# Packed attention and two expert layers on one core: a shorter float64 conversion and a four-turn attention pipeline

## The chip, the cores and the metric

The kernel runs on one core of one Trainium2 chip. The metric is the device time of one execution in microseconds (us). Engines are named as the profile names them: PE (TensorE), DVE (VectorE), ACT (ScalarE), POOL (GpSimd) and SP (SyncE, which issues the transfers). Each works through its own instructions in order and waits on semaphores for the others.

## What is computed

Three blocks in a row: attention over 32 learned queries p, a dense two-layer block with squared ReLU, and a block of eight experts of which each token takes one. The shapes are B = 8, H = 8, S = 576, D = 64 (4608 tokens of 512 values), `w_in` 512x2048, `w_out` 2048x512.

```python
def sm_attn(qq, kk, vv):
    s = scale * np.matmul(qq, kk.transpose(0, 1, 3, 2))
    s = s - np.max(s, axis=-1, keepdims=True)
    a = np.exp(s)
    a = a / (np.sum(a, axis=-1, keepdims=True) + 1e-09)
    return np.matmul(a, vv)
p_packed = sm_attn(p, k, v)
out = sm_attn(q, p_packed, p_packed)
x = out.transpose(0, 2, 1, 3).reshape(B * S, H * D)
h = np.maximum(x @ w_in, 0.0)
x = (h * h) @ w_out
# then: e = argmax(x @ w_gate + modality_bias), out = gate * (relu(x @ w1[e]) @ w2[e])
```

`w_in` and `w_out` arrive as float64. Each value is two 32-bit words, an upper (`top`: sign, exponent, the upper part of the fraction) and a lower one (`low`). The chip's engines work in float32, so the kernel puts each float32 together from these two words.

## The kernel before

**Stages.** A start loop takes 16 quads of heads through the first attention (`att1`: scores L297, maximum L308, exponential L310, normalisation L315, transposes L320/L321, their copies `atbuf` L322/L323, products `pq` L329/L330, results to `pp32` and split into two halves for PE by ACT L346 and POOL L347). Beside it 16 conversions turn `w_in` into `wbt`, and `pw_unit` (PE L361, copied out by DVE L365 or ACT L367, for the first pair split again by ACT L376 and POOL L377) multiplies the packed values with `w_in`. Then `others(u)` makes the rest of these products and converts `w_out`, one of 16 blocks per call, into the places of `wbt` that fall free. From there twelve units u of 384 tokens run, each with 16 steps f: `layer1` (PE L474, or L480/L482/L483 with DVE L487 for the four units that lie in two batches; then ACT L489 to L491 and a subtraction L493 make the two halves `ghl`), and `layer2` (PE L500, nine matmuls a step). The gate (L521) and the routing run behind them, and then the expert block, which the change does not touch.

**Conversion.** `convert` uses a scratch of two halves, m and tf, of which there are three, so conversion i takes the scratch that conversion i-3 used. In tf the float32 is built; ACT rounds it into the high half (L215), and POOL subtracts for the low half (L216). The raw words lie in three or four buffers; the transfer for a later block starts when the last DVE instruction that reads the buffer is done.

**Second attention.** `att2(u)` is a generator: for each of three tiles of 128 tokens it computes scores (PE L428) and subtracts the maximum (DVE L439), turn; exponential (ACT L443), sum and reciprocal (DVE L445 to L447) and multiplication (POOL L448) on the buffer `e`, of which there is one, turn; two transposes (PE L455) and the split into `a2T` (ACT L458, DVE L459), turn. In the units, `bga = Paced([att2(u + 1)], R_ATT)` takes R_ATT turns of it in each of the 16 steps.

**What sets the order.** The code is written in program order, and a planner arranges each engine's instructions by that order, by priorities (`CHAIN` puts L486 to L493 forty places ahead) and by a timeline that it simulates. So where an instruction stands on its engine can't be read from the code; the orders below are those of the built programs. Line numbers of the changed kernel are 2 lower from the end of `convert` on, and 1 lower from the new `yield` on; in its `convert`, L202 is the first ACT instruction, L203 the new maximum, L204 the mask and shift, L213 and L214 are what were L215 and L216.

Of the kernel before, what the change touches and what calls it, by code (L numbers as in the profile page):

```python
# [10 lines left out]
F32 = mybir.dt.float32  # L11
# [4 lines left out]
AF = mybir.ActivationFunctionType  # L16
ALU = mybir.AluOpType
# [2 lines left out]

P = 128
EPS = 1e-9
MIN_NORMAL = float(np.array([897 << 20], np.int32).view(np.float32)[0])


@with_exitstack
def tile_pack_attention_moe_moe2(
# [15 lines left out]
    nc = tc.nc  # L43
# [153 lines left out]

    def convert(sc, raw, hi, lo):
        top, low = raw[:, :, 1], raw[:, :, 0]
        m, tf = sc[:, :512], sc[:, 512:]  # L200
        t = tf.bitcast(I32)
        nc.scalar.activation(out=m, in_=top.bitcast(F32), func=AF.Square)  # L202
        nc.vector.tensor_scalar(  # L203
            out=t, in0=top, scalar1=0x07FFFFFF, scalar2=3, op0=ALU.bitwise_and, op1=ALU.logical_shift_left  # L204
        )
        nc.vector.scalar_tensor_tensor(
            out=t, in0=top, scalar=-0x40000000, in1=t, op0=ALU.bitwise_and, op1=ALU.bitwise_or
        )
        nc.vector.scalar_tensor_tensor(
            out=t, in0=low, scalar=29, in1=t, op0=ALU.logical_shift_right, op1=ALU.bitwise_or  # L210
        )
        nc.vector.scalar_tensor_tensor(
            out=tf, in0=m, scalar=MIN_NORMAL * MIN_NORMAL, in1=tf, op0=ALU.is_ge, op1=ALU.mult  # L213
        )  # L214
        nc.scalar.activation(out=hi, in_=tf, func=AF.Copy)  # L215
        nc.gpsimd.tensor_tensor(out=lo, in0=tf, in1=hi.bitcast(F32), op=ALU.subtract)  # L216
# [12 lines left out]
    def conversions(srcs, raws, scs):  # L229
        n = len(raws)  # L230

        def load(i):
            if i < NU:
                nc.sync.dma_start(raws[i % n].bitcast(I32).rearrange("p (f t) -> p f t", t=2), srcs[i])

        for i in range(n):
            load(i)
        for i in range(NU):
            w = wbt[:, i]
            raw = raws[i % n].bitcast(I32).rearrange("p (f t) -> p f t", t=2)  # L240
            convert(scs[i % len(scs)], raw, w[:, 0, :], w[:, 1, :])
            load(i + n)
            yield
# [12 lines left out]
    def bank(tag, name):  # L256
        if "early" in held:
            return held["early"].tile([P, 512], F32, tag="e", name=name, bufs=4)
        return held["all"].tile([P, 512], F32, tag=tag, name=name, bufs={"acc": 3, "h": 2, "t": 3}[tag])
# [148 lines left out]
    def parts(t0, n):  # L408
        got, t = [], t0
        while t < t0 + n:  # L410
            b = t // S
            e = min(t0 + n, (b + 1) * S)
            got.append((b, t - t0, e - t))
            t = e
        return got

    def att2(u):
        hl = held["at"].tile([P, 2, NPC, UW], F32R, tag="a2T", name="a2T", bufs=2)
        a2T[u] = hl
        for r in range(UT):  # L420
            t0 = u * UW + r * P
            c0 = r * P
            qT = held["at"].tile([P, HP, P], F32, tag="qT", name="qT", bufs=2)
            nc.sync.dma_start(qT, qT_d[:, t0 : t0 + P].rearrange("(g p) t -> p g t", p=P))
            s2 = bank("t", "s2")
            for b, off, n in parts(t0, P):
                for g in range(HP):
                    nc.tensor.matmul(  # L428
                        s2[off : off + n, g * 64 : (g + 1) * 64],
                        qT[:, g, off : off + n],  # L430
                        pp32[:, b, g, :],
                        start=True,
                        stop=True,
                    )
            s2v = s2[:, : H * NPK].rearrange("p (h n) -> p h n", h=H)
            mx = held["at"].tile([P, H], F32, tag="mx", name="mx", bufs=2)
            nc.vector.tensor_reduce(out=mx, in_=s2v, axis=AX.X, op=ALU.max)
            e = held["at"].tile([P, H, NPK], F32, tag="e", name="e", bufs=1)
            nc.vector.tensor_tensor(  # L439
                out=e, in0=s2v, in1=mx.unsqueeze(2).to_broadcast([P, H, NPK]), op=ALU.subtract  # L440
            )
            yield
            nc.scalar.activation(out=e, in_=e, func=AF.Exp, scale=SCALE)  # L443
            sm = held["at"].tile([P, H], F32, tag="sm", name="sm", bufs=2)
            nc.vector.tensor_reduce(out=sm, in_=e, axis=AX.X, op=ALU.add)  # L445
            nc.vector.tensor_scalar(out=sm, in0=sm, scalar1=EPS, scalar2=None, op0=ALU.add)
            nc.vector.reciprocal(out=sm, in_=sm)  # L447
            nc.gpsimd.tensor_tensor(  # L448
                out=e, in0=e, in1=sm.unsqueeze(2).to_broadcast([P, H, NPK]), op=ALU.mult
            )  # L450
            yield
            ta = bank("t", "ta2")
            ef = e.rearrange("p h n -> p (h n)")
            for c in range(NPC):
                nc.tensor.transpose(ta[:, c * P : (c + 1) * P], ef[:, c * P : (c + 1) * P], ident)  # L455
            tv = ta[:, : NPC * P].rearrange("p (c n) -> p c n", c=NPC)
            hi = hl[:, 0, :, c0 : c0 + P]
            nc.scalar.activation(out=hi, in_=tv, func=AF.Copy)  # L458
            nc.vector.tensor_tensor(out=hl[:, 1, :, c0 : c0 + P], in0=tv, in1=hi.bitcast(F32), op=ALU.subtract)  # L459
            yield  # L460
# [418 lines left out]
                    split_pw(b, i)  # L879


    R_ATT = 0.75
    pT_v = pT_d.rearrange("p (b g n) -> p b g n", b=B, g=HP)
    nc.sync.dma_start(pn[:, :2], pT_v[:, :2])
    load_k(0)
# [9 lines left out]
    for i in range(len(quads) + 3):  # L895
        if i < len(quads):
            runs.append(att1(i))
        for r in (runs if i < 3 else runs[:1] + runs[:0:-1]):
            with tc.high_priority(offset=PRI):
                next(r)  # L900
        if i >= 3:
            runs.pop(0)
        if i == A20:
            bg = [att2(0)]
        pull(bg)
        pull(cv, 2)
        if i == 8:
            pull(cv, NU)
            held["head"] = const.tile([P, HEAD, 2, NPC, P], F32R, tag="head", name="head")
        for bp, u in PW.get(i, ()):  # L910
            pw_unit(bp, u)
# [54 lines left out]
    for u in range(NUN):  # L966
        pair, k = divmod(u, UPP)
        last = u == NUN - 1
        if u == 1:
            st1.close()  # L970
            nc.sync.dma_start(
                wgb.rearrange("p e d -> p (e d)"), w_gateT.rearrange("e d -> (e d)").partition_broadcast(P)
            )
            held["xg"] = ctx.enter_context(tc.tile_pool(name="xg", bufs=2, side="right"))
        bga = Paced([] if last else [att2(u + 1)], R_ATT)
        for f in range(NF):
            hl = layer1(u, f)
            if pend is not None:
                second_layer()
            pend = (u, f, hl)  # L980
            if f == 0:
                gens, n = background(u)
                bgt = Paced(gens, n / ((NF - 6 if last else NF) - 1.5))
            if u == 0:
                others(f + AHEAD)
            bga.step()
            bgt.step()
            ahead(pair, k, f)
            if last and f == NF - 6:
                bgt.finish()  # L990
                bgt = Paced([weights1(0)], 1)
        bga.finish()
        bgt.finish()
# [74 lines left out]
```

## Time and profile before

| | |
|---|---|
| median of 3 runs | 1283.46 us (1280.68 to 1285.04) |
| the profiled execution | 1291.58 us |
| its span, first to last instruction | 1289.7 us |
| PE busy | 1235.6 us, 96% |
| DVE busy | 834.3 us, 65% |
| ACT busy | 633.3 us, 49% |
| POOL busy | 325.2 us, 25% |

The profiled execution took 0.6% longer than the median, and 1.9 us of its time lie outside its span. PE is busy nearly everywhere, but not at the same pace: in the page's forty slices the granted clock of TensorE is 0.6 to 0.7 of full speed in the first four and 0.8 or more in the others. A busy share counts what an engine is occupied with, also where an instruction takes longer because something else stands in its way.

### The profile page before, as it was taken

To read this page: it belongs to the slowest core of one execution; us is meant where nothing else is said; L and a number is where in the kernel's file an instruction comes from. 1 tells how busy PE (TensorE), PEld (TensorE's weight loads), DVE (VectorE), ACT (ScalarE), POOL (GpSimd) and SP (SyncE) were. 2 spreads that over 40 slices of the span, in tenths; PEclk is the share of its full clock that TensorE was granted. 3 is DMA by queue.
4 is the path that set the end of the run, shared out by engine and by line. 5 is a ranking of instruction groups with operands and counts; after the bars stand their busy time and mean duration, and the time that the engine had idled before them with its cause. 6 is when DMAs were issued, how large, how long until landed. Compare 5 with 4: busy or idle time off the path is not lost.

```text
span 1289.7 us, 18073 instructions
## 1 busy us (share of the span) xinstructions
PE 1235.6 (96%) x6100; PEld 1021.7 (79%) x6100; DVE 834.3 (65%) x2168; ACT 633.3 (49%) x1337; POOL 325.2 (25%) x389
## 2 busy tenths in 40 slices
PE   7898989899999999999999999999999999999995
PEld 5566878688888888888888888878787888888884
DVE  4877676687685985779597497988643454354331
ACT  3556466466546765456754576642332333343230
POOL 3644365332101222013221023101220121122011
PEclk6777999999999999999999999999999999999998
DMA  9875665621111222012220112341542442353210
GB/s 335 281 267 185 185 180 176 180 83 50 59 50 33 67 74 67 9 53 74 64 72 20 43 40 87 99 156 42 181 135 90 170 167 97 131 182 115 97 66 36
DMA packets 74167, 145.04 MB, mean 112 GB/s; under 512 B 6608, under 2 KB 26192, under 8 KB 73936
## 3 DMA queue, kind: packets, MB, share of 16 engines
q1 hardware_dynamic: 68304, 124.62, 29.8%
q0 software_dynamic: 5760, 19.17, 4.6%
q8 instruction: 50, 0.82, 0.3%
q14 instruction: 53, 0.43, 0.1%
HBM read 109.92 MB, written 33.85 MB: 111 GB/s over the span
## 4 chain that ended last, share of the span: by engine, by line
PE 74%; DVE 10%; DMA 6%; issue 4%; ACT 2%; POOL 2%; SPq 0%; POOLq 0%; DVEq 0%; ACTq 0%
PE acc L500 24%; PE o L809 13%; PE h L787 12%; PE ph L474 9%; DMA wraw<-in_moe_w 3%; DVE rows L521 3%; PE pq L329 3%; PE pw L361 2%; PE s L428 2%; PE s L297 1%; PE ph L482 1%; PE ph L483 1%; PE ph L480 1%; PE tr L767 1%; DMA wgb<-in_moe_w_gate 1%
## 5 line engine op out<-in xcount | busy, mean ns | idle before, releaser
L500 PE MATMUL acc<-wbt,ghl 128*128 128x512 f32 x1728 | 446.0, 399 | 2.6 <-ACT ghl L491 2.3
L500 PEld LDWEIGHTS acc<-wbt,ghl 128*128 128x128 f32 x1728 | 319.5, 189 | 64.4 <-ACT ghl L491 4.3
L521 DVE SCALAR_TENSOR_TENSOR rows<-rows,wgb 128x512 f32<-128x512 f32 x288 | 213.8, 742 | 6.8 <-DMA wgb<-in_moe_w_gate 3.4
L787 PE MATMUL h<-xt,wbt 128*128 128x512 f32 x864 | 214.2, 398 | 0.4 <-DVE xt L771 0.4
L787 PEld LDWEIGHTS h<-xt,wbt 128*128 128x128 f32 x864 | 162.2, 189 | 39.6 <-DVE xt L771 0.9
L493 DVE TENSOR_TENSOR ghl<-r,ghl 128x384 fp32r<-128x384 f32 x176 | 107.0, 610 | 78.2 <-ACT ghl L491 76.4
L491 ACT ACTIVATE ghl<-r 128x384 fp32r<-128x384 f32 x192 | 99.9, 521 | 82.7 <-PE acc L500 80.8
L820 POOL DMA_INDIRECT out<-wgb,idx_s x36 | 39.2, 1088 | 341.1 <-DVE wgb L818 251.4
L798 DVE SCALAR_TENSOR_TENSOR ht<-h,ht 128x512 fp32r<-128x512 f32 x72 | 48.8, 687 | 113.3 <-ACT ht L797 112.2
L809 PE MATMUL o<-head,ht 128*128 128x512 f32 x432 | 113.8, 398 | 4.8 <-ACT ht L797 4.5
L809 PE MATMUL o<-ring,ht 128*128 128x512 f32 x432 | 111.5, 394 | 0.0
L797 ACT ACTIVATE ht<-h 128x512 fp32r<-128x512 f32 x72 | 42.0, 592 | 140.2 <-PE h L787 139.9
L490 ACT ACTIVATE r<-r 128x384 f32<-128x384 f32 x192 | 99.7, 523 | 4.1
L809 PEld LDWEIGHTS o<-head,ht 128*128 128x128 f32 x432 | 80.6, 189 | 24.7 <-ACT ht L797 5.8
L809 PEld LDWEIGHTS o<-ring,ht 128*128 128x128 f32 x432 | 80.5, 188 | 17.0
L489 ACT ACTIVATE r<-ph 128x384 f32<-128x384 f32 x128 | 61.9, 486 | 63.2 <-PE ph L474 34.7
L405 POOL TENSOR_TENSOR ring<-praw,ring 128x256 fp32r<-128x256 f32 x62 | 51.1, 825 | 156.3 <-ACT ring L404 138.4
L474 PE MATMUL ph<-a2T,ring 128*128 128x384 f32 x420 | 85.6, 339 | 0.0
L474 PEld LDWEIGHTS ph<-a2T,ring 128*128 128x128 f32 x420 | 74.7, 188 | 4.8
L724 DVE TENSOR_TENSOR wbt<-wraw,wbt 128x1024 fp32r<-128x1024 f32 x36 | 44.0, 1223 | 51.0 <-ACT wbt L723 50.5
L474 PE MATMUL ph<-a2T,head 128*128 128x384 f32 x348 | 72.5, 340 | 0.0
L448 POOL TENSOR_TENSOR e<-e,sm 128x256 f32<-128x256 f32 x36 | 28.7, 797 | 171.1 <-DVE sm L447 164.6
(225 smaller groups left out, 1860.3 us busy)
## 6 DMA issues: line engine op xcount, KB each, us to landing
wraw<-in_moe_w SPq DMA_DIRECT2D x72, 512.0 KB, 3.6
praw<-pw_d SPq DMA_DIRECT2D x56, 256.0 KB, 3.8
pw_d<-pws SPq DMA_DIRECT2D x48, 256.0 KB, 3.2
x_d<-rows SPq DMA_DIRECT2D x12, 792.0 KB, 4.2
qT<-in_q SPq DMA_DIRECT2D x36, 256.0 KB, 3.0
early<-in_v SPq DMA_DIRECT2D x16, 512.0 KB, 5.5
rows<-in_k SPq DMA_DIRECT2D x10, 576.0 KB, 7.0
wgb<-in_moe_w_out SPq DMA_DIRECT2D x11, 512.0 KB, 4.1
```

The lines of the kernel that those rows point to most:

```text
L405: nc.gpsimd.tensor_tensor(out=t[:, 1], in0=raw, in1=t[:, 0].bitcast(F32), op=ALU.subtract)
L474: nc.tensor.matmul(ph, t[:, x, c, :], a[:, y, c, :], start=(i == 0), stop=(i == 3 * NPC - 1))
L489: nc.scalar.activation(out=r, in_=ph if len(ps) == 1 else r, func=AF.Relu)
L490: nc.scalar.activation(out=r, in_=r, func=AF.Square)
L491: nc.scalar.activation(out=hl[:, 0], in_=r, func=AF.Copy)
L493: eng.tensor_tensor(out=hl[:, 1], in0=r, in1=hl[:, 0].bitcast(F32), op=ALU.subtract)
L500: nc.tensor.matmul(acc[t], hl[:, x, t * P : (t + 1) * P], wbt[:, f, y, :], start=(f == 0 and x == 0 and y == 0), stop=(f == NF - 1 and x = ...
L521: nc.vector.scalar_tensor_tensor(out=junk, in0=row[:, t, :DM], scalar=1.0, in1=wgb[:, e], op0=ALU.mult, op1=ALU.mult, accum_out=one)
L724: nc.vector.tensor_tensor(out=t[:, 1, :], in0=raw, in1=t[:, 0, :].bitcast(F32), op=ALU.subtract)
L787: nc.tensor.matmul(ph, half1[:, g % 2, c, x, f * P : (f + 1) * P], xs[c][:, y, :], start=(i == 0), stop=(i == 3 * NDC - 1),)
L798: nc.vector.scalar_tensor_tensor(out=h[:, 1, :], in0=ph, scalar=0.0, in1=h[:, 0, :].bitcast(F32), op0=ALU.max, op1=ALU.subtract)
L809: nc.tensor.matmul(po, hs[f][:, x, t * P : (t + 1) * P], second(f)[:, y, :], start=(i == 0), stop=(i == 3 * NFE - 1),)
```

## The change

Three edits. In `convert`, ACT writes the absolute value of the upper word (read as a float) into tf, where it wrote the square into m; a new DVE instruction takes the maximum of that and a constant (in place); the mask and shift now read tf in place of the strided upper word; and the last DVE instruction, which multiplied the result by a comparison of the square with a limit, is dropped. So DVE still has four instructions for a block, a maximum in place of the comparison, and ACT's comes at the head of the chain. In `att2` a second `yield` stands between the multiplication and the transposes, so a tile has four turns and not three. `R_ATT` goes from 0.75 to 0.95 turns a step.

```diff
-MIN_NORMAL = float(np.array([897 << 20], np.int32).view(np.float32)[0])
+TOP_MIN = float(np.array([896 << 20], np.int32).view(np.float32)[0])
...
-        m, tf = sc[:, :512], sc[:, 512:]
+        tf = sc[:, 512:]
         t = tf.bitcast(I32)
-        nc.scalar.activation(out=m, in_=top.bitcast(F32), func=AF.Square)
+        nc.scalar.activation(out=tf, in_=top.bitcast(F32), func=AF.Abs)
+        nc.vector.tensor_scalar(out=tf, in0=tf, scalar1=TOP_MIN, scalar2=None, op0=ALU.max)
         nc.vector.tensor_scalar(
-            out=t, in0=top, scalar1=0x07FFFFFF, scalar2=3, op0=ALU.bitwise_and, op1=ALU.logical_shift_left
+            out=t, in0=t, scalar1=0x07FFFFFF, scalar2=3, op0=ALU.bitwise_and, op1=ALU.logical_shift_left
         )
...
-        )
-        nc.vector.scalar_tensor_tensor(
-            out=tf, in0=m, scalar=MIN_NORMAL * MIN_NORMAL, in1=tf, op0=ALU.is_ge, op1=ALU.mult
         )
         nc.scalar.activation(out=hi, in_=tf, func=AF.Copy)
...
                 out=e, in0=e, in1=sm.unsqueeze(2).to_broadcast([P, H, NPK]), op=ALU.mult
             )
+            yield
             yield
             ta = bank("t", "ta2")
...
-    R_ATT = 0.75
+    R_ATT = 0.95
```

The first place is ACT during the conversions of `w_in`, where the fifth block is worked on (`stage`, `wgb` and `extra` are raw buffers and scratches; `atbuf` is the copy of the transposed scores, `abuf` the exponentials). Before:

```order
L202 ACTIVATE stage<-wgb 128x512
L215 ACTIVATE wbt<-stage 128x512
L202 ACTIVATE stage<-extra 128x512
L202 ACTIVATE wgb<-stage 128x512
L322 ACTIVATE atbuf<-ta 128x512
L310 ACTIVATE abuf,sm<-s_391,mx 128x576
```

Now:

```order
L202 ACTIVATE stage<-wgb 128x512
L202 ACTIVATE stage<-extra 128x512
L202 ACTIVATE wgb<-stage 128x512
L320 ACTIVATE atbuf<-ta 128x512
L308 ACTIVATE abuf,sm<-s_391,mx 128x576
L213 ACTIVATE wbt<-stage 128x512
```

The rounding into `wbt`, which stood second and needs the whole DVE chain, has moved behind the copy `atbuf` and the next exponential.

The second place is ACT during the conversions of `w_out` (`pws` is the copy of a product out of PSUM, `ring` its high half for PE, `r` and `ghl` are the steps of unit 0). Before:

```order
L215 ACTIVATE wbt<-rows 128x512
L491 ACTIVATE ghl<-r 128x384
L202 ACTIVATE wgb<-wgb 128x512
L367 ACTIVATE pws<-pw 128x512
L376 ACTIVATE ring<-pws 64x4x128
L367 ACTIVATE pws_1354<-pw 128x512
L489 ACTIVATE r<-ph 128x384
```

Now:

```order
L213 ACTIVATE wbt<-rows 128x512
L490 ACTIVATE ghl<-r 128x384
L202 ACTIVATE rows<-rows 128x512
L365 ACTIVATE pws<-pw 128x512
L374 ACTIVATE ring<-pws 64x4x128
L365 ACTIVATE pws_1354<-pw 128x512
L213 ACTIVATE wbt<-wgb 128x512
```

The first instruction of a conversion (L202) stands as before a place or two behind a rounding and ahead of the copies `pws`; it now writes tf, so it waits for POOL's subtraction that follows such a rounding, which it did not before.

The third place is PE in unit 1, where a tile of the second attention is transposed (`ta`) and the scores `s` of the next one follow. Before:

```order
L480 MATMUL ph<-a2T,head 128x384
L482 MATMUL ph<-a2T,head 128x192 x2
L483 MATMUL ph<-a2T,head 128x384
L455 MATMUL ta_2378<-ident,e 128x128 x2
L428 MATMUL s_2451<-pp_85,qT 128x64 x4
L500 MATMUL acc<-wbt,ghl 128x512 x9
```

Now:

```order
L479 MATMUL ph<-a2T,head 128x384
L481 MATMUL ph<-a2T,head 128x192 x2
L482 MATMUL ph<-a2T,head 128x384
L454 MATMUL ta_2411<-ident,e 128x128 x2
L426 MATMUL s_2451<-pp_85,qT 128x64 x4
L499 MATMUL acc<-wbt,ghl 128x512 x9
```

The transposes stand where they stood: behind the same step of the first layer and right ahead of the next tile's scores.

## Rows read from the trace of the kernel before

**Rows 1.** Busy time by stage: window, us, five engines (x), PEclk, DMA share, GB/s

```profile
0.00:45.00 45.00, 30.67 (x136) 21.32 (x136) 25.88 (x61) 18.60 (x37) 22.43 (x51) 0.66 0.93 316
45.00:95.00 50.00, 49.05 (x262) 35.45 (x262) 38.47 (x99) 28.08 (x61) 26.72 (x29) 0.79 0.83 282
...
145.00:233.00 88.00, 83.98 (x401) 69.64 (x399) 65.84 (x93) 54.21 (x109) 55.02 (x43) 0.98 0.60 180
...
260.00:795.00 535.00, 531.36 (x2806) 458.72 (x2805) 403.18 (x1270) 322.09 (x764) 112.09 (x135) 1.00 0.19 56
```

**Rows 2.** Waits of PE, 0 to 112 us: us in total, times, longest

```profile
PE pq L329 <- ACT atbuf L322: 5.1, 4, 3.6
PE s L297 <- ACT abuf L310: 4.7, 2, 2.7
```

**Rows 3.** Timeline of ACT at 39 to 45 us: start, us, instruction, idle before

```profile
39.47 0.66 ACT L202 ACTIVATE stage<-wgb 128x512 f32<-128x512 f32 x1
43.10 0.63 ACT L215 ACTIVATE wbt<-stage 128x512 fp32r<-128x512 f32 x1 [2.97 <-DVE stage L212]
43.64 0.65 ACT L202 ACTIVATE stage<-extra 128x512 f32<-128x512 f32 x1
...
44.74 0.58 ACT L322 ACTIVATE atbuf<-ta 128x512 f32<-128x512 f32 x1
```

**Rows 4.** Timeline of PE at 39 to 46 us

```profile
39.86 1.06 PE L320 MATMUL ta<-ident,abuf 128*128 128x128 f32 x4
...
45.38 0.69 PE L329 MATMUL pq<-atbuf,early 128*128 128x64 f32 x2 [3.63 <-ACT atbuf L322]
```

**Rows 5.** Conversion instructions by line: ns min/median/max, first and last start

```profile
L202 ACT ACTIVATE wgb<-wgb x13: 647/670/689, 21.0 to 206.1; 128x512 f32<-128x512 f32 x13
...
L203 DVE TENSOR_SCALAR wgb<-wgb x13: 410/428/1504, 20.8 to 217.4; 128x512 int32<-128x512 int32 x13
...
L212 DVE SCALAR_TENSOR_TENSOR wgb<-wgb x17: 673/692/1777, 24.3 to 220.2; 128x512 f32<-128x512 f32 x17
```

**Rows 6.** Chain of work that ended last, 100 to 112 us: start, us, what

```profile
104.62 1.25 POOL wbt L216
...
105.90 0.44 DVE wgb L203
...
106.36 1.66 DVE wgb L206
...
109.79 1.57 DVE wgb L212
```

**Rows 7.** Timeline of POOL in the same stretch

```profile
105.94 4.87 POOL L377 TENSOR_TENSOR head<-pws,head 64x512 fp32r<-64x512 f32 x3
```

**Rows 8.** The chain from 145 to 205 us, its lines' shares and two pieces

```profile
by line: DMA wgb<-in_moe_w_out 14.2%; issue 12.2%; DVE wgb L209 11.8%; DVE wgb L206 8.3%; DMA rows<-in_moe_w_out 6.7%; DVE wgb L203 6.0%; DVE pws L365 5.0%; DVE rows L212 4.6%; POOL wbt L216 4.5%; DVE wgb L212 4.3%; DMA pw_d<-pws 3.9%; ACT 
...
148.44 1.25 DVE wgb L203
...
187.14 0.44 DVE wgb L203
```

**Rows 9.** Waits of DVE, 145 to 233 us

```profile
DVE wgb L203 <- POOL wbt L216: 10.8, 5, 4.8
DVE rows L203 <- POOL wbt L216: 3.9, 2, 2.0
```

**Rows 10.** Waits of ACT, 145 to 233 us

```profile
ACT wgb L202 <- DMA wgb<-in_moe_w_out: 9.4, 6, 2.6
```

**Rows 11.** Waits of PE, 112 to 260 us

```profile
PE pw L361 <- DVE pws L365: 3.3, 2, 2.3
PE ph L480 <- DVE r L487: 3.0, 3, 1.7
PE pw L361 <- ACT pws L367: 1.4, 2, 0.7
```

**Rows 12.** Waits of PE, whole run

```profile
PE ta L455 <- POOL e L448: 2.3, 4, 0.7
```

## The prediction, made before the changed kernel had run

> **What bounds the kernel now.** I read the busy time by stage first, then the waits of PE in the stages with room, then the timelines at the longest of those waits, and last the chain of work through the conversions. The table by stage [rows 1] parts the run. From 260 to 795 us, where the units run that hold most of the second attention, PE is busy 531.4 of 535 us: 3.6 us are all that anything there can win. In the first 45 us PE is busy 30.7 us, at a granted clock of 0.66, and the transfers fill 0.93 of the DMA engines' time. From 45 to 95 us PE is again full (49.05 of 50 us). From 145 to 233 us it is busy 84.0 of 88 us. So the change can win only in the first 260 us, around the conversions, and there only where PE waits for something that a conversion holds up. All 32 conversions lie there: the first start of their instructions is at 21 us and the last at 220 [rows 5].
>
> Two waits of PE in the start loop are for ACT: 5.1 us for the copy `atbuf`, of which 3.6 in one place, and 4.7 us for exponentials [rows 2]. The long one shows how a conversion comes in. ACT issues L202 at 39.47 us and then stands at the rounding L215 for 2.97 us until DVE has done L212; two more L202 follow, and only at 44.74 the copy `atbuf` [rows 3]. Its input had been written by the transposes from 39.86 on, 1.06 us long, so it was there at 40.9; PE waits 3.63 us for the copy [rows 4].
>
> **Term A: the order of ACT in the start loop.** The built order takes the rounding out of that place: three L202 follow each other, then the copy, then the exponential, then the rounding. Starts of neighbouring ACT instructions of this size are 0.54 us apart (43.10 to 43.64) [rows 3], so the copy is reached at 39.47 + 3 x 0.55 = 41.1 us, and its input is there. That is 3.6 us earlier than 44.74. I take -3.4, since PE's wait of 3.63 cannot go wholly: the copy still lies between transposes and product. The ends: -3.6, and 0 if the next transfer sets the pace, which a share of 0.93 makes possible [rows 1]. The stall at the exponentials (4.7 us) stays: in the order the two roundings ahead of it stand where they stood.
>
> **Term B: DVE's shorter conversion and its new first link.** Dropped is L212, median 0.692 us. The new maximum does not occur in this trace. Its nearest row is L203, a tensor_scalar of the same 128x512, median 0.428; the upper end is the dropped instruction's own 0.692 [rows 5]; a gain beyond 0.428 has no reason, since L203's shortest is 0.410. I take 0.43, the same kind of instruction: 0.26 us for each of 32, 8.4 us of DVE. Little of that is on a path. In the chain from 145 to 205 us L212 holds 4.6 + 4.3 = 8.9% of 60 us, or 5.3 us [rows 8]; cut in the ratio 0.26 to 0.69 that is -2.0. Against it stands the new link. Before, DVE's L203 was the instruction that wrote into tf first and had to wait for POOL's L216 of the conversion three earlier; ACT's square wrote m and ran aside. Now ACT's absolute value waits for it, and DVE's maximum waits for ACT. Wherever L216 releases the conversion and this is on the chain, an ACT instruction of 0.67 us [rows 5] comes in. The chain passes straight from L216 to L203 in four places: at 105.90 [rows 6], and in the later stretch in three, of which 148.44 is the first and 187.14 the last [rows 8]. Four times 0.67 is +2.7. The sum of the two is +0.7; ends -2.0 (the Abs hides behind other waits) and +2.7.
>
> What the maximum costs beside POOL is weighed here. At 105.90 L203 took 0.44, and the next DVE instructions 1.66 and 1.57 us in place of 0.69 [rows 6], while POOL ran L377, three instructions from 105.94 on [rows 7]. L203 itself goes up to 1.50 in other places [rows 5], so a tensor_scalar is not spared. The Trainium skill (SBUF — State Buffer, section "Who interferes with whom") says that a DVE instruction with two inputs in SBUF, and one in a two-port mode such as a tensor_scalar, shares ports with GpSimd, and that the later one blocks for the whole instruction. By that rule the maximum wins nothing where POOL is busy, and by the share of POOL from 145 to 233 us, 55 of 88, the 2.0 us above would be 0.75 and the sum of term B +1.9; the trace agrees as far as the 1.50 shows.
>
> **Term C: products from 112 to 233 us.** PE waits 3.3 us for DVE's copies L365 and 1.4 us for ACT's L367 [rows 11]. Both stand in a queue with conversion work. DVE's lighter load and the end of its own waits (below) shorten the first; the second may grow. I take -2, ends -3.3 and 0 here; growth is the rival below.
>
> **Term D: att2.** The new turn and the rate go together: 9 turns at 0.75 are taken by step 12 of 16, 12 turns at 0.95 by step 13, so `a2T` is complete one step later and still before the next unit's first L474, with two steps in hand. The wait that the turn aims at, PE's transposes for POOL's L448, is 2.3 us in the whole run, in four places [rows 12]. The built order says that the planner had already put the transposes well behind, and puts them now into the same place, in front of the next tile's scores: since `e` and the turns bind the tile's steps to each other, one turn more in the code is not one step more on PE. Where the order differs, the distance grows at some tiles and shrinks at as many. I take 0; ends -2.3 and +2.3, the same again.
>
> **The sum.** -3.4 + 0.7 - 2 + 0 = -4.7 us. Against the profiled execution of 1291.58 us that is 1286.9. The median of the runs is 0.6% lower, 1283.46, and the difference is carried over as it stands: 1278.8, so 1279.
>
> **Rivals.**
>
> *Slower: ACT takes over the waits for POOL.* From 145 to 233 us DVE waits 10.8 + 3.9 = 14.7 us at L203 for POOL's L216, seven times [rows 9]. The wait does not vanish; it moves to ACT's L202, which in the built order stands right behind the rounding that POOL's subtraction follows. Behind it in ACT's queue are the copies `pws` and their splits, and L489 to L491 of unit 0, for which PE's L361 and L500 wait. For the rival: ACT has no fourth scratch, and its order was not rearranged to give L202 more room. Against it: ACT waits 9.4 us at L202 already, for the raw words [rows 10], and the two waits overlap in part. If under 4.7 of the 14.7 us reach PE, the forecast's gain is left in part; at 4.7 it is gone; from 4.7 + 3.9 = 8.6 us the kernel is measurably slower. At three quarters, 11 us, it is 1283.5 - 4.7 + 11 = 1290.
>
> *More than forecast.* If the early order shifts the exponentials too, both waits of rows 2 go, 9.8 us, and with a lighter DVE the 3.0 us that PE waits at L480 for L487 at the end of the stretch [rows 11]: -12.8, so 1270.5. For it: all these waits are for engines that convert. Against it: most of the other waits' places have kept their order.
>
> *Nothing comes through.* The gain at 41 to 45 us lies ahead of a stretch in which PE is full and the transfers take 0.83 of the DMA engines' time [rows 1]. If the next keys or raw words set the pace, what PE gains at 45 us it waits for them, and the rest balances as terms B and D do: 1283.
>
> **How the numbers follow.** A run of this kernel can tell 0.3%, 3.9 us, from no change. The forecast, 1276 to 1282, has 0.45 (0.32 of it beyond 3.9 us, 0.13 within). More than forecast, about 1270: 0.14. Nothing: 0.18. Slower, about 1290: 0.23 (0.21 beyond, 0.02 within). So faster 0.46, same 0.33, slower 0.21. The range takes the gain of the second rival with 2 us more, 1268, and the slower one up to 1291, where 11 of the 14.7 us have come through; beyond these lie about 2 in 10.
>
> **What would show it.** Term A: PE's longest wait for `atbuf` under 1 us in the first 60 us, and the copy ahead of the rounding. Term B: the maximum at 0.41 to 0.45 us where POOL is idle, and DVE's waits for L216 gone from its list, since ACT holds them. Term C and the slower rival: the list of ACT's waits from 145 to 233 us names POOL's subtraction at L202; if it sums to under 5 us and PE's waits for `pws` shrink, the forecast holds; if PE's waits there exceed 4.7 us, the rival does. Term D: PE's wait for the multiplication between 1 and 4 us. From 260 to 795 us the span should stay within 2 us; if that stretch moves more, my reading of the turns was wrong.

## The result and the profile after

| | before | after |
|---|---|---|
| median | 1282.64 us (1280.68 to 1285.04, 4 runs) | 1292.52 us (1289.92 to 1293.83, 4 runs) |
| the profiled execution | 1291.58 us | 1292.91 us |
| its span | 1289.7 us | 1291.1 us |

The ratio is 1.0074, interval 1.0049 to 1.0098: slower by 0.7%, where 1279 was forecast and the range ended at 1291. Twelve further runs (after_again below) gave 1.0036 (1.0009 to 1.0063); the two intervals overlap, and the mean of the two ratios is 1.0055. Ratios compare the executions within 1.5% of the fastest of their kernel; in conv_only below this leaves out three of twelve, all above 1295 us.

The two profiled executions differ by 1.3 us only, since the one of before lies 9 us above its own median. A third profile of that kernel (below) shows where most of that lies: executions of one program differ in the clock that TensorE is granted in the first 100 us. So what follows compares stages, and the verdicts come from the timed comparisons.

The table by stage of the changed kernel (window, us, five engines, PEclk, DMA share, GB/s), to be read against [rows 1]:

```profile
0.00:45.00 45.00, 32.98 (x157) 23.32 (x157) 25.36 (x66) 20.83 (x42) 21.31 (x54) 0.77 0.98 341
45.00:95.00 50.00, 47.08 (x269) 33.15 (x268) 39.40 (x101) 30.43 (x62) 21.11 (x27) 0.86 0.85 282
95.00:112.00 17.00, 9.07 (x33) 7.14 (x31) 14.35 (x18) 9.64 (x16) 14.39 (x11) 0.63 0.28 85
...
145.00:233.00 88.00, 84.84 (x414) 70.90 (x413) 66.83 (x95) 59.11 (x115) 52.19 (x44) 1.00 0.61 187
...
260.00:795.00 535.00, 530.13 (x2788) 456.84 (x2787) 404.41 (x1269) 322.64 (x762) 108.84 (x132) 1.00 0.18 55
```

The same line of the kernel before, which [rows 1] leaves out:

```profile
95.00:112.00 17.00, 12.09 (x59) 7.79 (x58) 12.21 (x22) 11.48 (x22) 11.90 (x9) 0.75 0.44 134
```

PE does more in the first 95 us (157 + 269 matmul records against 136 + 262), and then works only 9 of 17 us, where it worked 12. From 260 to 795 us it is full as before.

ACT at 38 to 43 us, the place of term A (compare [rows 3]):

```profile
38.23 0.66 ACT L202 ACTIVATE stage<-wgb 128x512 f32<-128x512 f32 x1
38.79 0.67 ACT L202 ACTIVATE stage<-extra 128x512 f32<-128x512 f32 x1
39.36 0.65 ACT L202 ACTIVATE wgb<-stage 128x512 f32<-128x512 f32 x1
39.91 0.59 ACT L320 ACTIVATE atbuf<-ta 128x512 f32<-128x512 f32 x1
...
42.77 0.62 ACT L213 ACTIVATE wbt<-stage 128x512 fp32r<-128x512 f32 x1
```

The copy comes at 39.91 and not at 44.74. Of these 4.8 us the first L202 accounts for 1.2, since it is that much earlier too; counted from it, the copy comes 3.6 us sooner. The waits of PE from 0 to 112 us (compare [rows 2]):

```profile
PE pw L359 <- ACT pws L365: 7.4, 1, 7.4
...
PE s L295 <- ACT abuf L308: 5.3, 2, 4.0
...
PE pq L327 <- ACT atbuf L320: 1.0, 2, 0.6
```

The wait for `atbuf` fell from 5.1 to 1.0 us, and a new one of 7.4 us stands at the first products with `w_in`. Its place, on PE and on ACT:

```profile
93.83 1.19 PE L295 MATMUL s<-rows,ptb 128*64 128x288 f32 x8
102.47 1.65 PE L359 MATMUL pw<-wbt,pphl 128*128 128x512 f32 x3 [7.45 <-ACT pws L365]
```

```profile
98.59 0.63 ACT L213 ACTIVATE wbt<-wgb 128x512 fp32r<-128x512 f32 x1 [3.60 <-DVE wgb L210]
99.13 1.92 ACT L374 ACTIVATE head<-pws 64x512 fp32r<-64x512 f32 x3
```

```profile
97.87 0.69 DVE L210 SCALAR_TENSOR_TENSOR wgb<-stage,wgb 128x512 int32<-128x512 int32 x1
```

PE can go on when the buffers `pws` are emptied into `head`. `head` is declared with the same tag as `stage`, so it lies in the memory in which the blocks of `w_in` are converted, and its first instruction comes when the last block is out of it: 99.13 us here, behind the last DVE instruction that reads `stage` (the L210 above). In the three profiles of before it comes 0.3 us behind the last such read: at 99.98, 100.55 and 95.21 us. So the lead of the start loop ends there; against the third profile, whose clock from 64 to 80 us was 1.00 as here (below), it has turned into 3.9 us of delay.

Waits of ACT and then of DVE from 145 to 233 us (compare [rows 9, 10]):

```profile
ACT wgb L202 <- DMA wgb<-in_moe_w_out: 2.5, 2, 1.9
...
ACT rows L202 <- POOL wbt L214: 1.5, 1, 1.5
...
ACT wgb L202 <- POOL wbt L214: 0.3, 1, 0.3
```

```profile
DVE wgb L203 <- ACT wgb L202: 6.0, 5, 3.1
DVE rows L203 <- ACT rows L202: 2.3, 1, 2.3
```

The wait for POOL did move to ACT, but it is 1.8 us there, not 14.7. The waits of PE from 112 to 260 us that term C was about (compare [rows 11]) fell from 3.3 + 1.4 to 2.3 + 0.7 us:

```profile
PE pw L359 <- DVE pws L363: 2.3, 2, 1.4
...
PE pw L359 <- ACT pws L365: 0.7, 1, 0.7
```

### The profile page after: what moved, and what is told of

It is laid out like the page before. It is cut to its first block, busy times and chain, and to the rows that moved or that the text cites. A ratio compares the mean times of both kernels' runs of the same rounds, so it can differ in the third digit from the quotient of the medians.

```text
span 1291.1 us, 18073 instructions
## 1 busy us (share of the span) xinstructions
PE 1237.7 (96%) x6100; PEld 1026.0 (79%) x6100; DVE 837.5 (65%) x2168; ACT 638.5 (49%) x1337; POOL 313.3 (24%) x389
## 4 chain that ended last, share of the span: by engine, by line
PE 79%; DVE 12%; DMA 3%; issue 2%; ACT 2%; POOL 0%; SPq 0%; POOLq 0%; ACTq 0%; DVEq 0%
PE acc L499 25%; PE h L786 15%; PE o L808 15%; PE ph L473 9%; DVE rows L520 4%; PE pw L359 3%; PE pq L327 2%; DMA wraw<-in_moe_w 2%; PE s L426 2%; PE s L295 1%; PE ph L481 1%; PE tr L766 1%; PE ph L482 1%; PE ph L479 1%; PE pq L328 1%
## 5 line engine op out<-in xcount | busy, mean ns | idle before, releaser
L499 PE MATMUL acc<-wbt,ghl 128*128 128x512 f32 x1728 | 446.3, 399 | 2.3 <-ACT ghl L490 1.7
L499 PEld LDWEIGHTS acc<-wbt,ghl 128*128 128x128 f32 x1728 | 318.9, 189 | 63.2 <-ACT ghl L490 3.0
L359 PE MATMUL pw<-wbt,pphl 128*128 128x512 f32 x192 | 57.4, 425 | 13.9 <-ACT pws L365 8.2
```

The costliest lines, as they stand in the source:

```text
L359: nc.tensor.matmul(ph, hl[:, x, hp], w[:, y, :], start=(i == 0), stop=(i == 2))
L499: nc.tensor.matmul(acc[t], hl[:, x, t * P : (t + 1) * P], wbt[:, f, y, :], start=(f == 0 and x == 0 and y == 0), stop=(f == NF - 1 and x = ...
```

## The experiments

Each profiled execution is cut into three here: to the end of the last L500 of unit 0; from there to the end of the last L500 of unit 11; from there to the end of the last L809, the last matmul of the expert block (us, read from the ends of these matmuls; the line numbers are those of the kernel before).

| kernel | its profiled time | to unit 0's end | units 1 to 11 | rest |
|---|---|---|---|---|
| before, first profile | 1291.6 | 234.9 | 623.6 | 417.9 |
| before_again | 1288.3 | 235.4 | 622.0 | 415.7 |
| before_third | 1282.1 | 229.1 | 622.3 | 415.4 |
| after | 1292.9 | 235.7 | 628.2 | 413.9 |
| after_again | 1287.3 | 233.2 | 625.1 | 413.9 |
| att_only | 1292.1 | 236.7 | 628.1 | 412.2 |
| att_units_only | 1285.2 | 230.2 | 627.6 | 412.3 |
| att_start_only | 1285.4 | 232.1 | 622.3 | 415.8 |
| yield_r10 | 1286.9 | 231.5 | 625.1 | 415.0 |
| rate_only | 1285.7 | 231.1 | 625.4 | 414.1 |
| yield_only | 1315.6 | 234.8 | 651.1 | 414.5 |
| conv_only | 1281.9 | 225.7 | 624.3 | 416.9 |
| conv_again | 1296.2 | 241.9 | 623.1 | 416.0 |
| conv_m | 1297.6 | 240.4 | 624.4 | 417.6 |
| after_r12 | 1285.5 | 229.0 | 625.3 | 415.9 |

The columns are not steady to the microsecond for one order. The first also holds the clock. The second holds unit 1, which takes 66.2 to 69.6 us whatever the order (after_again and after are one program: 625.1 and 628.2). And what PE loses in unit 11 it can win back behind: in the four profiles of the changed order it stands idle for 1.8 us in unit 11 and then waits 1.1 to 2.4 us for ACT's `ht` in the expert block; in the seven that have the order of before in the units it is 0.0 and 2.8 to 4.5. Two other cuts are steadier:

| order in the units | end of unit 1 to end of unit 10, us | unit 11 and rest together, us |
|---|---|---|
| as before (the three of before, att_start_only, conv_only, conv_again, conv_m) | 497.1 to 498.0 | 472.8 to 475.3 |
| as changed (after, after_again, att_only, att_units_only) | 498.4 to 498.9 | 472.3 to 475.4 |

By these the changed order costs about 1 us in units 2 to 10, and behind them no difference shows.

**The kernel before, two more profiles.** No edit.

> The kernel before, unchanged, for a second profile and more times, since its first profiled execution (1291.6 us) lies 9 us above its other runs. If that 9 us is the granted clock of TensorE in the first 150 us, the new profile is near 1282 us and shows PEclk above 0.92 from 112 to 145 us and a mean clock above 0.972. If the first profile was an odd execution for another reason (a transfer, a wait), the clock by stage is as in rows 1 and the gain lies in a wait. If executions simply differ by 10 us, the times here spread from 1281 to 1292.

> The kernel before once more, for a third profile. Its times fall into about 1281 and about 1287; if the two are told apart by the waits of the first expert groups (about 5 us of idle PE between 830 and 940 us in the two profiles so far, of 1291.6 and 1288.3 us), an execution near 1281 shows less than 2 us there; if by the start, its first unit ends before 231 us.

Medians of 1283.56 us (12 runs) and 1282.09 (one). The second of the two profiled executions is near the median and the first is not, and the difference lies before unit 0's end: 6.3 us there, 6.2 in all. The stretch from 64 to 80 us, in the first profile of before and in the third:

```profile
64.00:80.00 16.00, 15.42 (x56) 9.71 (x56) 11.61 (x29) 7.54 (x16) 8.50 (x8) 0.57 0.78 267
```

```profile
64.00:80.00 16.00, 15.42 (x105) 11.45 (x103) 14.34 (x39) 12.02 (x27) 10.25 (x9) 1.00 0.97 335
```

PE is equally busy in both; at a granted clock of 0.57 it gets through 56 matmuls and at 1.00 through 105; before_again is like the first (58 matmuls at 0.57). Of the 5.8 us by which unit 0 ends later in the first profile than in the third, the instructions of ACT, which are the same in both, fall behind by 5.7 between 65 and 81 us. It is the clock, as the first expectation said, though not from 112 to 145 us but from 64 to 80.

**The parts apart.** conv_only and conv_again have the edit in `convert` alone, att_only the other two edits alone.

> Only the conversion as changed; attention in three turns at 0.75. Theory: the whole loss is the conversion's, by the order it brings about in the first 150 us: 1288 to 1294, +6 to +10 us. Rival (the attention's turns cost it): 1278 to 1284, -4 to +1 us, since then the conversion's own gain of the start loop is left.

> Only the fourth turn and the rate of 0.95; conversion as before. Theory (the loss is the conversion's): 1280 to 1285, within 3 us of the kernel before, as term D had it. Rival (the turns cost it): 1288 to 1294, with waits of PE or a longer stretch from 235 to 800 us.

att_only: 1290.67 us, ratio 1.0051 (1.0025 to 1.0078). That was the rival's range, and its loss is clear of noise. conv_only: 1289.1 us, ratio 1.0013 (0.9975 to 1.0051), so no difference that can be measured, with single times from 1276 to 1296. Its median lies in the theory's range, but only because the times fall into two groups (below); the mean of all twelve lies 0.3% above that of the kernel before. So the theory that the conversion carries the whole loss fell: the attention alone loses as much as the changed kernel. Whether the conversion adds something, up to some 0.5%, these times can't tell.

**The turn without its rate.**

```diff
+            yield
             yield
             ta = bank("t", "ta2")
```

> Only the fourth turn, rate left at 0.75, so that the twelve turns take all 16 steps. Theory: the place of the transposes on PE hardly moves, within 3 us of the kernel before. Rival (late completion of the second attention is what costs): +4 us or more, with PE waiting for a2T at the units' first steps.

1316.44 us, ratio 1.0249 (1.0206 to 1.0292): the rival. Unit 11 alone takes 78.5 us in place of 57.4, with PE's wait from 800 to 830 us, and the last tile's transposes behind it:

```profile
PE pl L666 <- DVE od L658: 17.5, 1, 17.5
```

```profile
825.49 0.34 PE L666 MATMUL pl<-od,om 128*128 128x184 f16 x1 [17.51 <-DVE od L658]
825.62 0.63 PE L456 MATMUL ta<-ident,e 128*128 128x128 f32 x2
```

Twelve turns at 0.75 end with the unit's last step; the last tile is then late for the next unit, among the routing's work, which comes at the same place. So the end of unit 10 has no room to spare.

**The turn at the old places, and the rate alone.** yield_r10 has the second `yield` and `R_ATT = 1.0`, rate_only `R_ATT = 0.95` alone, after_r12 is the changed kernel with `R_ATT = 1.2`.

> Attention in four turns at a rate of 1.0, conversion as before. The twelve turns then end in step 12 of 16, and the transposes fall due in steps 4, 8 and 12, the same as in the kernel before; in the built order the last transposes of unit 10 stand ahead of the same step of the second layer as before (after 15 of 16), where the 0.95 puts them after the 16th. Theory (the 8.4 us of att_only are the lateness of the transposes at the ends of units, above all at the last): 1280 to 1286, within 3 us of the kernel before, with unit 11 back near 57.4 us from 61.4. Rival (the turn itself, or the other order that it brings about, costs wherever it stands): 1288 or more.

> Three turns as before, rate 0.95, so the nine turns end in step 10. Theory (lateness costs, earliness does not): 1279 to 1285, unit 11 near 57.4 us. Rival (the rate crowds the steps whatever the turns): 1288 or more.

> The changed kernel with a rate of 1.2: twelve turns in ten steps; the last transposes of unit 10 stand after 12.7 of 16 steps. Theory: the attention's loss is gone and what is left is the conversion as in conv_only, so times between 1276 and 1296 in two groups, the lower one near 1280 or under; unit 11 near 57.4 us. Rival (the two parts lose together for a reason of their own): 1290 or more in all executions.

yield_r10: 1287.6 us, 1.0046 (1.0030 to 1.0062). rate_only: 1285.68, 1.0014 (1.0000 to 1.0029). after_r12: 1285.6, 1.0022 (1.0006 to 1.0038). Unit 11 comes back from 61.5 us to 57.8, 55.3 and 53.9, as the theory said, but other units grow: units 4, 5 and 10 take 61.4, 54.0 and 59.0 us in yield_r10 against 59.4, 52.9 and 57.7 in before_third, and unit 10 takes 61.9 in rate_only and 61.1 in after_r12. In these two, part of unit 11's first layer has moved ahead of unit 10's end. From the end of unit 1 to the end of the expert block the three take 973.6, 973.4 and 971.6 us, against 970.6 to 974.4 in the four profiles of the changed order. So it is not shown that the units lose by lateness at their ends: the orders without it are not shorter in sum, and rate_only, whose turns only come earlier, has the longest units 2 to 10 of all, 504.0 us.

None of the three did what its theory said. yield_r10 lies above its range and just under the rival's; it also has the fourth turn in the start loop, which the next experiment prices. rate_only missed by 0.7 us. after_r12, with that turn too, has no two groups and nothing near 1280: 1283.9 to 1289.3.

**Units and start loop apart.**

```diff
+            if u:
+                yield
             yield
...
-    R_ATT = 0.75
+    R_ATT = 0.95
```

That is att_units_only; att_start_only has `if not u:` and the old rate. The first has the order of before up to 145 us, the second the order of before in the units.

> Four turns and the rate of 0.95 in the twelve units only; in the start loop the second attention of unit 0 keeps three turns, so the built order is the kernel before's up to 145 us. Theory (the attention's 8.4 us are two losses, about 2.6 us by late transposes in the units and the rest in the start loop): 1283.5 to 1286.5, with unit 11 at 61.5 us and the first unit's end between 229 and 235 us as in the kernel before. Rival (all of it lies in the units): 1288 or more.

> Four turns for unit 0 only, which the start loop pulls; units and rate as before, so the built order of the units is the kernel before's. Theory: 1286 to 1289, the first unit's end at 234 us or later in most executions, unit 11 at 57.4 us. Rival (the start is as before, and its spread is chance): 1281 to 1284.

> The changed kernel once more, on the same chip as the two parts. Theory: 1290 to 1294; the first unit's end at 234 us or later, with a granted clock under 0.8 from 105 to 130 us. Rival (its loss in the start was the chip's, not the order's): 1284 to 1289 here, as after_r12, whose built order is the same up to there, had elsewhere.

att_units_only: 1285.57 us, 1.0029 (1.0011 to 1.0047). att_start_only: 1286.01, 1.0028 (1.0008 to 1.0048), all but one of its twelve between 1284.5 and 1287.3; unit 0 ended at 232.1 us, sooner than expected and inside what the kernel before shows (229.1 to 235.4). The two parts add to 0.57%, 7.3 us, which is what att_only (0.51%) and the changed kernel (0.74 and 0.36%) lose within their intervals. In the start loop the transposes of unit 0's last tile come at 121.7 us in att_start_only and 94.5 in before_third; by which wait that costs time is not shown.

after_again: 1288.45 us, in the rival's range and not the theory's. Its times form two groups, six from 1284.5 to 1287.3 with a mean granted clock of 0.974 to 0.978 and six from 1289.6 to 1293.0 with 0.967 to 0.971; the four executions of the first comparison (1289.9 to 1293.8) have 0.968 to 0.973. So part of the distance between 0.74 and 0.36% is the clock. att_only's loss isn't: its times, 1288.6 to 1293.7, don't follow the clock, 0.967 to 0.982.

In the units the order differs most at the end of unit 10. The transposes of unit 11's last tile in the changed kernel and the step that uses them:

```profile
803.63 0.41 PE L454 MATMUL ta<-ident,e 128*128 128x128 f32 x2 [1.24 <-DVE xt L770]
...
805.67 2.63 PE L473 MATMUL ph<-a2T,head 128*128 128x384 f32 x8 [0.37 <-DVE a2T L458]
```

and the same transposes in the first profile of before:

```profile
797.74 0.38 PE L455 MATMUL ta<-ident,e 128*128 128x128 f32 x2
```

They come 5.9 us later (0.8 of which the changed profile is late at unit 0's end already), behind the unit's sixteenth step of L499 and twelve of the expert block's first transposes, where before they stood behind the fifteenth and three. PE waits for the copies `xt` of those transposes, and the first layer of unit 11 waits for the late tile in turn. Together with a third wait of 0.2 us these are the 1.8 us in unit 11; in after and att_only its clock is also 0.97 and not 1.00, which is why it takes 61.5 us there and 60.0 in after_again. The expert block then waits less for `ht`, and att_units_only's rest is 3.1 us shorter than before_third's (412.3 against 415.4); of the 5.3 us by which its units are longer 1.7 lie in unit 1. So in the profiles about 1 us of the units' 0.29% is located, in units 2 to 10; where the rest of it lies stays open.

**The conversion again, and with its wait put back on DVE.**

```diff
-        tf = sc[:, 512:]
+        m, tf = sc[:, :512], sc[:, 512:]
...
-        nc.scalar.activation(out=tf, in_=top.bitcast(F32), func=AF.Abs)
-        nc.vector.tensor_scalar(out=tf, in0=tf, scalar1=TOP_MIN, scalar2=None, op0=ALU.max)
+        nc.scalar.activation(out=m, in_=top.bitcast(F32), func=AF.Abs)
+        nc.vector.tensor_scalar(out=tf, in0=m, scalar1=TOP_MIN, scalar2=None, op0=ALU.max)
```

> The conversion alone once more. Its executions lay in two groups, 1276 to 1283 and 1291 to 1296. Theory: the upper group is a granted clock that stays low after PE's wait at 95 us, so a profile of that group shows 0.5 to 0.7 for over 30 us between 85 and 145 us and the first unit's end at 235 us or later, and one of the lower group 226 us. Rival: the upper group loses its time in the units or in the expert block.

> The conversion alone, with the absolute value written into the scratch's other half, as the square was; the maximum reads it from there and writes tf. So ACT's first instruction no longer waits for POOL's subtraction of the conversion three earlier, and DVE's maximum does. Attention as in the kernel before. Theory (the two groups of executions of conv_only and conv_again come from how TensorE is fed in the first 100 us by any conversion with this order of work, and the clock it is granted there, not from ACT's new wait): two groups again, about 1278 to 1283 and 1289 to 1296, or at least four of twelve over 1288. Rival (ACT's new wait makes the upper group): one group, 1277 to 1284.

conv_again: 1286.36 us, 1.0027 (0.9990 to 1.0064). This profile is one of the long executions, conv_only's one of the short ones; both are the same program. From 50 to 81 us, conv_only and then conv_again:

```profile
50.00:81.00 31.00, 30.42 (x204) 22.80 (x203) 27.62 (x74) 21.67 (x47) 17.03 (x21) 1.00 0.96 325
```

```profile
50.00:81.00 31.00, 30.53 (x116) 22.20 (x116) 16.10 (x47) 11.65 (x25) 9.94 (x13) 0.50 0.65 211
```

Nearly all of the 16.2 us between their first columns comes from here (ACT's same instructions fall behind by 14.7 us between 48 and 81 us): the clock stayed at 1.2 GHz in one and was at 2.4 in the other. My theory had put it after PE's wait at 95 us; it is earlier. The other executions agree: of the 24 of both runs, the eleven at 1291 us and more have a mean granted clock of 0.956 to 0.963, the eleven under 1284 have 0.970 to 0.980. Against before_third, whose clock was also at 1.00 from 64 to 80 us, conv_only reaches unit 0's end 3.4 us sooner, 225.7 against 229.1.

conv_m: 1293.58 us, 1.0082 (1.0059 to 1.0106): neither one low group nor two. Its waits of DVE from 138 to 236 us, and conv_only's from 138 to 222:

```profile
DVE wgb L203 <- POOL wbt L214: 15.6, 5, 4.9
DVE rows L203 <- POOL wbt L214: 8.5, 2, 4.3
```

```profile
DVE wgb L203 <- ACT wgb L202: 5.9, 3, 3.1
...
DVE rows L203 <- ACT rows L202: 1.6, 1, 1.6
```

From the first to the last rounding of a block of `w_out` it takes 95.1 us, conv_only 81.9 and conv_again 81.3, before_third 86.8. Putting the wait for POOL on DVE costs 13 us here; ACT is the better place for it. What makes the clock rise late in about half of the conversion's executions stays open: conv_m moved something else.

No version beat the kernel before in a measurable way.

## Why the prediction was wrong

**Term D is the step that failed.** It stood at 0, with ends of 2.3 us either way, and measured 0.51% in att_only and 0.57% as the sum of its two parts, some 7 us. It failed twice. The first is an omission: the new `yield` also counts in the start loop, which pulls the second attention of unit 0 once per quad, so that took twelve turns in place of nine there; I costed the turns in the units only. att_start_only puts that at 0.28% (0.08 to 0.48). The second, 0.29% (0.11 to 0.47) by att_units_only, is the reading of the order in the units: I showed a place in unit 1 where the transposes stay, and took the rest to balance on average. In the changed profile the last tiles of units 3, 5 and 9 are transposed behind 13 steps of the second layer instead of 9 or 10, and that of unit 11 behind the sixteenth, in the next unit's work. "With two steps in hand" was counted in turns of the code; the planner's order had none in hand at the end of unit 10, and before already stood after 15 of 16. yield_only shows what a tile costs that comes too late altogether, 21 us in unit 11; the smaller delay in the changed kernel costs 1.8 us in unit 11, but the expert block's shorter waits give as much back, so it is not shown that the units lose by it. My bound for the term was the wait that the turn was to take away (2.3 us), which can't bound what another order of the tiles costs.

That wait did shrink, from 260 to 795 us to

```profile
PE ta L454 <- POOL e L446: 0.5, 2, 0.2
```

from 1.5 us there, so the aim was met, beyond the 1 to 4 us that I had named as its sign. But PE's wait for L486 (L487 before) rose in the same stretch, from the first line to the second:

```profile
PE ph L480 <- DVE r L487: 0.7, 3, 0.3
```

```profile
PE ph L479 <- DVE r L486: 2.3, 5, 0.7
```

Units 2 to 10 grew by about 1 us, within the 2 us that were forecast for them.

**Term A was right in place and size, and did not last.** The copy came 3.6 us earlier counted from the L202 ahead of it, PE's wait for `atbuf` lost 4.1 us, and a quarter of the products `pq` was done at 48.5 us against 54.0 to 54.9. Between there and 95 us the lead held; at 95 us it ran into `head`. PE's wait for `pws` there is 7.4 to 7.5 us in after, after_again and after_r12, 4.0 and 5.0 in conv_only and conv_again, and none over 1 us in before, before_again and before_third, so the conversion brings it and the turns of the attention lengthen it. The rival "nothing comes through" had the outcome for the conversion alone, with another reason (transfers): the cause seen is the memory that `head` shares with `stage`. Its chance of 0.18 was too low, since I followed the gain only to the next stretch and did not ask where the loop's products have to be put. Behind the stop, with PE busy 0.55 of 8 us from 95 to 103, TensorE ran near half clock: from 103 to 128 us it was granted 0.52 (0.69 in after_again), against 0.78 and 0.93 in the first and third profile of before, where PE was busy 5.1 and 6.9 of those 8 us.

**Term C was right in size, and term B's added link did not cost what I charged.** The two waits of term C lost 1.7 us where I took -2. For term B, the maximum takes what L203 took:

```profile
L203 DVE TENSOR_SCALAR wgb<-wgb x17: 399/428/1523, 20.3 to 217.3; 128x512 f32<-128x512 f32 x17
```

The median is 0.428 as forecast, and beside POOL it goes up to 1.52 (at 154.4 us), so there it saves little over an L212, as weighed. The stretch from the first to the last rounding of `w_out` shrank from 86.9 to 83.2 us (first profiles), and to 81.9 in conv_only: -3.7 to -5.0 where B and C summed to -1.3. The added link that I charged with 2.7 us came with what helped: conv_m has the link too but leaves the wait for POOL on DVE, and its stretch is 13 us longer than conv_only's. A wait for POOL on ACT holds up less here than one on DVE. But that stretch began later, its first rounding at 148.8 us and not 144.3, after the stop at `head`. In sum the conversion alone is 1.0013 and 1.0027 with both intervals around 1. (The prediction let the conversions end at 220 us, the last start of one group of [rows 5]; the last rounding starts at 231.2. No term hangs on it.)

**The slower rival** had the sign and the size (1290) and not the mechanism: of the 14.7 us that were to move to ACT, 1.8 arrived. That its number was met is luck.

## What to carry to other kernels

A turn added to a generator is added wherever it is pulled: list every caller before costing it, and look at the last item of each round, which can fall behind the round's end even if the average place is the same; in yield_only that cost 21 us in one unit. Before a longer stage is called a loss, see whether the next one has grown shorter by as much. An early gain is worth what lies beyond the next buffer that is shared: follow it to the first tile that can't be written yet. Where an engine waits for another, the price depends on what is queued behind the waiting instruction, so moving a wait to another engine can be worth more than the instruction saved.

## What the runs showed of the hardware

The granted clock of TensorE differs between executions of one program in the first 100 us, by up to 31 us at half clock (0.50 against 1.00 from 50 to 81 us, with PE busy over 98% of both), and moved unit 0's end from 225.7 to 241.9 us. A single profile can therefore hide or feign a difference of 6 to 16 us in this stage: the first profile of before lay 9 us above its median, and its unit 0 ended 5.8 us later than in the third.

The same DVE maximum of 128x512 took 0.40 to 0.43 us where POOL was idle and up to 1.52 beside POOL.
